# One core, a long convolution and a dilated local attention: loads as streams of their own, exchanges on two queues, another last product, another end, another order

## The chip, the core and the metric

The kernel runs on one NeuronCore of a Trainium2 chip. The metric is the device time of one execution in microseconds (us); the median of several executions counts. Five engines work side by side, each through its own list of instructions in order: PE (matrix products, with weight loads beside them), DVE and ACT (elementwise work; here above all the copies that take results out of PSUM, called evictions below), POOL (small copies, and DMAs that it issues itself), and SP, which issues nearly all DMAs. An engine that waits holds back everything behind it in its list.

## The reference, cut to what matters

```python
def reference(A_q, A_k, A_v, A_shift_k, A_ssm_k, A_ssm_D, B_x, B_wqkv, B_wo, gate_w):
    x = A_q                                         # 1 x 2048 x 640, bf16
    g = sigmoid((x * gate_w).sum(-1, keepdims=True))
    # A: four taps along the sequence, times v, then a causal convolution of length 2048 (by FFT)
    kv = shift4(A_k, A_shift_k) * A_v
    y = causal_conv(kv, A_ssm_k) + kv * A_ssm_D
    a = A_q * y
    # B: 32 heads of 20; a query sees 8 keys, 2 apart
    q, k, v = split(x @ B_wqkv)
    b = softmax_over_8(q . k * 20 ** -0.5) . v @ B_wo
    return g * a + (1 - g) * b
```

## The kernel before

Branch B: `xpose` turns eight tiles of x (PE transposes into PSUM, then copies to `xT`). `vproj` multiplies `xT` with the value weights `Wv` (L522, 170 matmuls in 34 units of five, evicted to `VW`). `qkproj` multiplies with the query and key weights `Wqk` (L569, 45 units), 128 columns at a time (`ft` = 0 to 4), evicted into two staging tiles `stg` (queries, keys). A head has 20 columns, so the rows of a head must move to other partitions: `fragger` sends them by DMA, 20 rows each, from `stg` to the tiles `qb` and `kb` (L617). These are the exchanges. Four heads make a block (t = 0 to 7, in three pairs of `qb` and `kb`, filled with mask rows by POOL copies at the start). `score_gen` multiplies a block's queries and keys (L643), ACT takes the exponential (L651, into `ETall`), `pv_gen` multiplies with `VW` (L677), DVE divides (L687, L689). `op_tr` turns the result (L853, into `oT`), `outproj` multiplies with `wo` (L869) and scales by 1 - g out of PSUM into `bl` (L874 on ACT, L876 on DVE).

Branch A: `conv` and `conv_v` do the four taps and the product with v on DVE, in steps of eight of the 64 rows that a partition holds, from row 63 down. Two parts P = 0, 1 (half the channels each) then go through a transform of 2048 = 32 x 64 points: first step `s1_unit` (L705) and second step `s2_unit` (L721, with the table `G`), once for the kernel (`h`; P = 0 into H, P = 1 into SX; input tile `h_lin`, loaded twice) and once for kv (`u`; into UC and u1). `swaps` exchanges the halves of the kernel's transform by DMA (L820), `products` multiplies on DVE (L756), `inverse1` is the first step back (L835, evicted into UC), `final` the second (L920): for each unit of `TAIL` (first tile, number of tiles) 32 small matmuls a tile into two PSUM slots, evicted into `yb`, times the gated q (L932), plus `bl` (L934), and out by DMA (L937).

PSUM has four slots of two banks; a unit of PE work takes one (some half a slot, a score group and a final unit two) and gives it back when its eviction is done.

The order is written out by hand. Each piece of the program is a generator whose `yield Req(engines, cost, deps, ...)` marks one instruction or unit; the string `ORDER` names, letter by letter, the generator that goes next, and a "-" ahead of a letter takes the second of the engines offered. Costs and due times in the requests were used to find the string; they do nothing at run time. So `ORDER` alone decides in which order each engine's list is written, and whether ACT or DVE evicts. Before, the loads after the first ones are part of `fragger` (`bulk(ft)` runs when the exchanges of `ft` have been issued); `paced` makes a load wait for a small POOL memset of its target.

SP has eight completion semaphores in turn: each of its DMAs waits until the one eight earlier has landed.

Of the kernel before, what the change touches and what calls it, by code (L numbers as in the profile page):

```python
# [10 lines left out]
BF = mybir.dt.bfloat16  # L11
# [6 lines left out]
S = 2048  # L18
# [28 lines left out]
KROWS = [(42, 64), (20, 42), (0, 20)]  # L47
TAIL = [(0, 3), (3, 3), (6, 2), (8, 3), (11, 3), (14, 2)]
LAND = dict(W0=9600.0, Wv0=5600.0, W1=23000.0, Wv1=25500.0, x=[4200.0, 7000.0, 8100.0, 10700.0, 11800.0, 12900.0, 14000.0, 15200.0], k=[20300.0])
STARTS = dict(P=5000.0, A=5000.0, D=6500.0, G=12000.0, S=18000.0)  # L50
PIPE0 = 24500.0
# [64 lines left out]
a-aa-awa-w-aw-wwww-wa-aw-wai-i-aiiai-iaa-aaai-iiffiif-iiiiifffciwicccwwfwwww-wixccccccccccccccffw-ww-wwwwccccwcccccwcccfffwwwwwwwx  # L116
ifffi-idddi-iididi-iid-idi-ididdde-iddddifffiexxfxxiffccccccccccccceffxxxxxxxxxxffeffccccccccccccccccccccccciiicdcidddx-iddfci-xd
-iidddddfffccfxedciccccdixeffdiidii-idccccccccccccccccidicccccfddxefdd-xlidexdddeffffddxxddyxeffyyccccccccccccii-iiyiddieccfddddf
-iiddfedfx-x-iiiiidddiiiiddffffffyyyyedyyxfeeexyxyccxccccyyffy-yyyifyyccccx-x-icdccccdcciddfd-iiddg-ididdde-iddidddge-iccidedcdd-i
ie-iddgdi-iiddde-iddddccccgccjejy-yyyy-yyeyyeyy-yyyy-ycyjyy-yccccccyyccclcccccjdddzdd-zdzd-zdzdj-zz-zzzjczzcz-zccddzdzz-zjzzeddddd  # L120
ezd-zz-zz-zddzdde-zeddzd-zddeddde000-0000-00p0z0z-0zz0-0000-00e0ezzz-zzzz-z010-111111-11011-0101ooo-0q111111-1r-rroorr-rr-r001ruoo
10oo-r01-111000-000001ssss1ssssss000011ssssosssosss111o1oopooo1sssu1sssss11111122oso22222222o2oo324443uu3s44s3333333334vs444444u44
444-4445-5u-u555-55u-u-uu5vv5-5555v-u-vvv-55555-vvv5-5ttstss-tsvs-vstttt-ttssststtttssststttttts-ssssstttt-tttssssttssttstsstssst
# [91 lines left out]
def kernel(  # L215
# [117 lines left out]

    def load_k(k):
# [20 lines left out]
    def load_v(c, q):  # L355
        yield from paced(f"v{q}{c}", vin[32 * q:32 * q + 32, c], raw(v2, QC * q + 80 * c, [[64 * D, 32], [D, 64], [1, 80]]), 2550.0)
# [621 lines left out]
```

## Time and profile before

| what | value |
|---|---|
| median of 3 executions | 221.87 us (221.81 to 224.73) |
| the profiled execution, whole | 222.59 us |
| its span, first to last instruction | 220.8 us |
| mean granted TensorE clock | 0.973 |
| moved by DMA | 33.40 MB, of it 19.59 MB read from HBM and 2.62 MB written |
| first exponential starts | 34.38 us |
| first output transpose (L853) starts | 151.21 us |
| first matmul of `final` (L920) starts | 196.22 us |

The last three come from the timeline. Durations of single instructions overlap a little with the next one on the same engine: two exponentials in a row take 1.86 us, one alone 0.98 us. "Busy" counts such a stretch once.

### The profile page before, as it was taken

How to read it: one execution, taken by the hardware profiler on the slowest of the kernel's cores; microseconds unless marked ns; L12 is line 12 of the kernel's file. 1: busy time of each engine (PE TensorE's matmuls, PEld its weight loads, DVE VectorE, ACT ScalarE, POOL GpSimd, SP SyncE). 2: the span in 40 equal slices, each digit the busy share in tenths (PEclk: the TensorE clock that was granted, in tenths of full speed). 3: DMA queues.
4: the chain of work that ended last, by engine and by line, in shares of the span. 5: the costliest groups of instructions: out<-in, count | busy, mean ns of one | idle time of the engine just before them, and what ended most of it. 6: DMA issues, size and time to landing. Idle time of an engine off the chain costs nothing.

```text
span 220.8 us, 8196 instructions
## 1 busy us (share of the span) xinstructions
PE 200.2 (91%) x3498; PEld 150.5 (68%) x3508; DVE 184.5 (84%) x233; ACT 174.5 (79%) x242; POOL 52.9 (24%) x130
## 2 busy tenths in 40 slices
PE   7899999999999999999967958999999999979790
PEld 3666674664656557455765747888899999968680
DVE  4556984899999999988987798997899998969782
ACT  0334448848999999989897888998799999988671
POOL 6992621470544137041600000000010000000000
PEclk9999999999999999999995599999999999999998
DMA  6999569999999999997359854026757490003545
GB/s 200 343 257 289 138 157 204 175 172 156 197 167 177 180 164 148 177 157 138 77 109 272 240 132 116 12 54 173 172 122 162 83 223 17 4 3 91 137 117 139
DMA packets 69047, 33.40 MB, mean 151 GB/s; under 512 B 51348, under 2 KB 66708, under 8 KB 69012
## 3 DMA queue, kind: packets, MB, share of 16 engines
q1 hardware_dynamic: 65684, 27.66, 60.8%
q0 software_dynamic: 2880, 4.90, 10.1%
q8 instruction: 27, 0.44, 0.9%
q10 hardware_dynamic: 448, 0.33, 0.4%
q14 instruction: 8, 0.07, 0.1%
HBM read 19.59 MB, written 2.62 MB: 101 GB/s over the span
## 4 chain that ended last, share of the span: by engine, by line
PE 61%; DVE 12%; ACT 9%; DMA 6%; issue 6%; SPq 2%; POOL 2%; ACTq 0%; DVEq 0%
PE PS L569 16%; PE PS L869 9%; PE PS L677 7%; PE PS L835 6%; PE PS L522 6%; ACT ETall L651 5%; PE PS L643 4%; DVE SX L244 4%; DVE UC L244 3%; PE PS L721 3%; PE PS L705 3%; PE PS L853 3%; DMA xn<-in_A_q_dram 2%; DMA h_lin<-in_A_ssm_k_dram 2%; PE PS L920 2%
## 5 line engine op out<-in xcount | busy, mean ns | idle before, releaser
L651 ACT ACTIVATE ETall<-PS 128x976 bf16<-128x976 f32 (+3 forms) x80 | 63.5, 859 | 6.2 <-PE PS L643 5.2
L569 PE MATMUL PS<-xT,Wqk 128*128 128x512 bf16 (+2 forms) x215 | 47.9, 356 | 1.3 <-ACT ETall L651 0.5
L569 PEld LDWEIGHTS <-Wqk 128*128 128x128 bf16 x225 | 20.8, 97 | 18.6 <-issue 0.3
L242 ACT CAST UC<-PS 128x1024 bf16<-128x1024 f32 (+2 forms) x27 | 25.6, 1013 | 1.8 <-PE PS L721 1.1
L470 DVE TENSOR_TENSOR KX<-KX 128x1280 bf16<-128x1280 bf16 x32 | 25.3, 820 | 1.6 <-DMA KX<-in_A_k_dram 1.2
L522 PE MATMUL PS<-WvT,xT 128*128 128x320 bf16 x170 | 25.8, 300 | 0.1
L869 PE MATMUL PS<-wo,oT 128*128 128x320 bf16 x160 | 24.1, 303 | 0.0
L244 DVE CAST stg<-PS 128x512 bf16<-128x512 f32 (+1 forms) x25 | 16.1, 646 | 9.1 <-PE PS L569 7.7
L617 POOL DMA_DIRECT2D qb<-stg x29 | 14.5, 503 | 35.0 <-ACT ETall L651 11.8
L617 POOL DMA_DIRECT2D kb<-stg x36 | 18.0, 508 | 19.5 <-ACT stg L242 10.1
L869 PEld LDWEIGHTS <-oT 128*128 128x128 bf16 x160 | 21.0, 145 | 1.0
L721 PEld LDWEIGHTS <-G 64*128 64x128 bf16 x512 | 18.4, 93 | 4.0 <-issue 3.2
L522 PEld LDWEIGHTS <-xT 128*128 128x128 bf16 x170 | 16.0, 98 | 7.0
L677 PEld LDWEIGHTS <-ETall 128*128 128x128 bf16 x544 | 17.5, 99 | 2.4 <-issue 0.5
L643 PE MATMUL PS<-qb,kb 31*128 31x120 bf16 (+1 forms) x544 | 16.0, 222 | 2.8 <-ACT ETall L651 1.2
L677 PE MATMUL PS<-VW,ETall 128*128 128x63 bf16 (+2 forms) x544 | 18.0, 187 | 0.6 <-ACT ETall L651 0.3
L244 DVE CAST UC<-PS 128x1024 bf16<-128x1024 f32 (+1 forms) x14 | 16.5, 1206 | 2.2 <-ACT UC L242 1.4
L643 PEld LDWEIGHTS <-kb 31*128 31x128 bf16 x544 | 9.3, 95 | 12.7 <-issue 11.3
L242 ACT CAST VW<-PS 128x320 bf16<-128x320 f32 x23 | 9.8, 432 | 9.5 <-PE PS L522 9.1
L242 ACT CAST stg<-PS 128x512 bf16<-128x512 f32 (+1 forms) x20 | 10.9, 555 | 8.0 <-PE PS L569 7.1
L244 DVE CAST SX<-PS 128x1024 bf16<-128x1024 f32 (+2 forms) x13 | 14.4, 1156 | 2.6 <-PE PS L705 2.2
L874 ACT ACTIVATE bl<-PS,omg 128x320 bf16<-128x320 f32 x31 | 15.6, 540 | 0.8 <-PE PS L869 0.3
(83 smaller groups left out, 364.4 us busy)
## 6 DMA issues: line engine op xcount, KB each, us to landing
xn<-in_A_q_dram SPq DMA_DIRECT2D x8, 320.0 KB
h_lin<-in_A_ssm_k_dram SPq DMA_DIRECT2D x16, 160.0 KB
vin<-in_A_v_dram SPq DMA_DIRECT2D x8, 320.0 KB
UC<-H SPq DMA_DIRECT2D x8, 320.0 KB
q<-in_A_q_dram SPq DMA_DIRECT2D x8, 320.0 KB
w<-SX SPq DMA_DIRECT2D x8, 320.0 KB
kb<-stg POOLq DMA_DIRECT2D x28, 85.0 KB, 5.5
out_dram<-q SPq DMA_DIRECT2D x16, 120.0 KB
```

The source lines that it names most:

```text
L242: nc.scalar.copy(dst, src)
L244: nc.vector.tensor_copy(dst, src)
L470: eng.tensor_tensor(d, kin[:, n + 3 - j:n + 3 - j + m, :], w.to_broadcast([128, m, QC]), ALU.mult)
L522: nc.tensor.matmul(ps[:, 0:320], lhsT=xT[:, dt, BQ * b:BQ * b + BK], rhs=Wv[:, dt, 320 * hp:320 * hp + 320], start=(dt == 0), stop=(dt == ...
L569: nc.tensor.matmul(ps[:, 0:n], lhsT=Wqk[:, dt, w, 128 * ft:128 * ft + 128], rhs=xT[:, dt, s0:s0 + n], start=(dt == 0), stop=(dt == NDT - 1))
L617: (nc.sync if near else nc.gpsimd).dma_start(dst[r0:r0 + rows, 0:wd], stg[fa - f0:fb - f0, 0:wd])
L643: nc.tensor.matmul(psum(g, h4 // 2)[:, h4 % 2, QB[b][0] - q0:QB[b][0] - q0 + QB[b][1]], lhsT=kb[r:r + DH + NF, BK * b:BK * b + 128], rhs=q ...
L651: nc.scalar.activation(ETall[:, e, :, 0:nq], psum(g, k)[:, :, 0:nq], ACT.Exp, scale=SCALE)
L677: nc.tensor.matmul(O[:, (b - b0) // 6, c0:c0 + 21 * nh], lhsT=ETall[:, e, hh, q0:q0 + 128], rhs=VW[:, b, 4 * t + h4:4 * t + h4 + nh, :].re ...
L721: nc.tensor.matmul(ps[:, c, 160 * jj:160 * jj + 160], lhsT=G[rows, j0 + jj, 64 - 64 * rr:192 - 64 * rr], rhs=Am[rows, rr].rearrange("p o ( ...
L869: nc.tensor.matmul(op, lhsT=oT[:, ft].rearrange("p h m a -> p a (h m)")[:, t, :], rhs=wo[:, ft, 320 * n:320 * n + 320], start=(ft == 0), s ...
L874: nc.scalar.activation(dst, op, ACT.Copy, scale=omg[:, t:t + 1])
```

## The change

Five edits and a new order.

1. The loads leave `fragger`: `bulk` is gone, and x from its third tile on, the weights, k, h, G and v are streams of their own, which `ORDER` can place. Only two tiles of x, half of `Wv` and `mm` are issued ahead of it, `mm` on SP instead of ACT. k comes in six pieces of rows instead of three. The taps' weights come in one DMA instead of four.
2. The exchanges of all but the first queries may go to POOL or SP (`Req("GS", ...)`); before, they were POOL's.
3. `final`: only the first bank of a unit (half of the 640 channels) is evicted to `yb`, by ACT, and multiplied with q afterwards. The other is multiplied with q straight out of PSUM by DVE, in place of a copy by ACT or DVE and half of the larger product.
4. `TAIL`'s last unit of two tiles becomes two units of one. Their results leave by two DMAs each, of 64 partitions, one from SP and one from ACT, in place of four.
5. `outproj` works on whole tiles: ten matmuls into one slot and one eviction of 640 columns, in place of twice five and 320.

```diff
-KROWS = [(42, 64), (20, 42), (0, 20)]
-TAIL = [(0, 3), (3, 3), (6, 2), (8, 3), (11, 3), (14, 2)]
+KROWS = [(53, 64), (45, 53), (37, 45), (29, 37), (13, 29), (0, 13)]
+FIRST = 4
+TAIL = [(0, 3), (3, 3), (6, 2), (8, 3), (11, 3), (14, 1), (15, 1)]
...
 ORDER = """
-a-aa-awa-w-aw-wwww-wa-aw-wai-i-aiiai-iaa-aaai-iiffiif-iiiiifffciwicccwwfwwww-wixccccccccccccccffw-ww-wwwwccccwcccccwcccfffwwwwwwwx
+upppqqa-aaaa-a66ap6-aapp-a6666-6i-iiiaatti-ia-aat-aiirfiiitt4ii-ii-iiit6-6fff65t6rc-cc-ccc6-6666-666ccc66666v-6f6t666-cccc6cd66idd
...
+    def load_x():
+        for a in range(2, 8):
+            yield from load(f"x{a}", xn[:, a], raw(x2, 256 * a * D, [[2 * D, 128], [D, 2], [1, D]]), 1150.0)
...
-            yield from paced(f"k{k}{q}", kin[32 * q:32 * q + 32, 3 + n0:3 + n1, :], raw(k2, n0 * D + QC * q, [[64 * D, 32], [D, n1 - n0], [1, QC]]), 62.0 * (n1 - n0))
+            yield from (paced if k >= FIRST else load)(f"k{k}{q}", kin[32 * q:32 * q + 32, 3 + n0:3 + n1, :], raw(k2, n0 * D + QC * q, [[64 * D, 32], [D, n1 - n0], [1, QC]]), 48.0 * (n1 - n0))
...
-    def bulk(ft):
...
+    def load_ks():
+        yield from load("wr", wraw.rearrange("p c j -> p (c j)"), raw(A_shift_k, 0, [[4 * QC, 4], [0, 32], [1, 4 * QC]]), 560.0)
+        for k in range(len(KROWS)):
+            yield from load_k(k)
+        yield from load_corners()
...
+    def load_h1():
+        yield from load_h(1)
...
-                    g = yield Req("G", 510.0, deps, move=28.0 * rows)
-                (nc.sync if near else nc.gpsimd).dma_start(dst[r0:r0 + rows, 0:wd], stg[fa - f0:fb - f0, 0:wd])
+                    g = yield Req("GS", dict(G=510.0, S=760.0), deps, move=28.0 * rows)
+                (nc.sync if g.eng == "S" else nc.gpsimd).dma_start(dst[r0:r0 + rows, 0:wd], stg[fa - f0:fb - f0, 0:wd])
...
-            yield from bulk(ft)
...
+            g = yield Req("P", 0.0, [ev(f"oT{ft}") for ft in range(NDT)], take=1, pe=(10, 135.0, 272.0, 133.0))
+            op = psum(g)[:, :, 0:320]
             for n in range(2):
-                g = yield Req("P", 0.0, [ev(f"oT{ft}") for ft in range(NDT)], take=1, half=1, pe=(5, 137.0, 272.0, 133.0))
-                op = psum(g)[:, 0:320]
...
-                r = yield Req("AD", dict(A=370.0, D=400.0), [g.done], give=g.banks)
-                dst = bl[:, t, 320 * n:320 * n + 320]
...
+            r = yield Req("AD", dict(A=690.0, D=790.0), [g.done], give=g.banks)
+            dst = bl[:, t].rearrange("p (n c) -> p n c", n=2)
...
-            es = []
-            for k in range(2):
-                r = yield Req("AD", n=320 * m, deps=[g.done, ybfree[n % 2]], give=[g.banks[k]])
...
-            nc.vector.tensor_tensor(reg, yb[:, 0:m, :], reg, ALU.mult)
+            a = yield Req("A", n=320 * m, deps=[g.done, ybfree[n % 2]], give=[g.banks[0]])
+            nc.scalar.copy(yb.rearrange("p t (q c) -> p q t c", q=2), pss[0][:, :, 0:160 * m].rearrange("p q (t c) -> p q t c", c=160))
...
+            hi = reg[:, :, 320:640].rearrange("p t (q c) -> p q t c", q=2)
+            nc.vector.tensor_tensor(hi, pss[1][:, :, 0:160 * m].rearrange("p q (t c) -> p q t c", c=160), hi, ALU.mult)
+            r = yield Req("D", 75.0 + 0.52 * 320 * m, [a.done])
+            nc.vector.tensor_tensor(reg[:, :, 0:320], yb, reg[:, :, 0:320], ALU.mult)
...
+            if m == 1:
+                for k, e in enumerate((nc.sync, nc.scalar)):
+                    e.dma_start(raw(outf, (32 * k + 2 * t0) * D, [[D, 2], [64 * D, 32], [1, D]]), reg[64 * k:64 * k + 64, 0])
+                continue
             for gg in range(4):
-                (nc.scalar if n == len(TAIL) - 1 and gg > 1 else nc.sync).dma_start(raw(outf, (32 * (gg // 2) + gg % 2 + 2 * t0) * D, [[64 * D, 32], [2 * D, m], [1, D]]),
+                nc.sync.dma_start(raw(outf, (32 * (gg // 2) + gg % 2 + 2 * t0) * D, [[64 * D, 32], [2 * D, m], [1, D]]),
```

What the order does is shown at three places. Names in the rows are tiles; the number behind a name tells tiles of one shape apart (stg_92 holds queries, stg_93 keys). A trailing "x4" counts rows that repeat.

ACT, up to the first exponentials (`ETall`), in the kernel before:

```order
L242 CAST stg_93<-PS 128x384 x2
L242 CAST stg_92<-PS 128x512
L242 CAST stg_93<-PS 128x512
L242 CAST VW<-PS 128x16x20 x10
L242 CAST stg_92<-PS 128x512
L651 ACTIVATE ETall<-PS 128x2x488 x2
```

The same place in the changed kernel:

```order
L244 CAST stg_93<-PS 128x384 x2
L244 CAST stg_92<-PS 128x512
L244 CAST stg_93<-PS 128x512
L244 CAST VW<-PS 128x16x20 x8
L655 ACTIVATE ETall<-PS 128x2x488 x2
L655 ACTIVATE ETall<-PS 128x2x480 x2
```

Two evictions of `VW` and one of `stg` now come after the first exponentials; on PE the first scores stand behind 80 `vproj` and 45 `qkproj` matmuls instead of 90 and 55.

SP, in the kernel before, from the last loads of v to the first swaps (`UC<-H`); `h_lin` here is the second load of the convolution's kernel, `g_nat` the way of the gate through a DMA:

```order
L326 DMA vin<-in_A_v_dram 32x64x80 x5
L326 DMA h_lin<-in_A_ssm_k_dram 32x40x64 x6
L544 DMA g_nat<-WvT 32x1x16
L326 DMA h_lin<-in_A_ssm_k_dram 32x40x64 x2
L544 DMA g_nat<-WvT 32x1x16 x3
L326 DMA SX<-cf_T 128x4x512
L820 DMA UC<-H_288 64x5x512 x2
```

The same place in the changed kernel:

```order
L622 DMA qb_81<-stg_92 8x2056
L328 DMA h_lin<-in_A_ssm_k_dram 32x40x64
L622 DMA qb_83<-stg_92 20x2056 x2
L622 DMA kb_80<-stg_93 20x2176
L622 DMA kb_82<-stg_93 20x2176 x4
L328 DMA h_lin<-in_A_ssm_k_dram 32x40x64 x7
L549 DMA g_nat<-WvT 32x1x16 x4
L824 DMA UC<-H_276 64x5x512 x2
```

The gate's DMAs now stand behind all loads of `h_lin`, and the last exchanges of the keys (`kb`) ahead of seven of the eight.

ACT at the end of the kernel before:

```order
L242 CAST yb_3512<-PS 128x2x3x160 x2
L874 ACTIVATE bl<-PS,omg 128x320 x2
L242 CAST yb_3512<-PS 128x2x3x160
L874 ACTIVATE bl<-PS,omg 128x320 x3
L242 CAST yb_3512<-PS 128x2x2x160 x2
L874 ACTIVATE bl<-PS,omg 128x320 x3
L937 DMA out_dram<-q_3296 32x2x640 x2
```

ACT at the end of the changed kernel:

```order
L930 CAST yb_3529<-PS 128x2x3x160
L930 CAST yb_3529<-PS 128x320
L878 ACTIVATE bl<-PS,omg 128x640
L942 DMA out_dram<-q_3275 2x32x640
L878 ACTIVATE bl<-PS,omg 128x640
L930 CAST yb_3529<-PS 128x320
L942 DMA out_dram<-q_3275 2x32x640
```

The store of the last unit but one now stands in ACT's list ahead of the last eviction of `bl` and the last of `yb`; the shape at the row's end, 2x32x640 in place of 32x2x640, is that of the target in HBM, outermost count first.

Elsewhere: 36 matmuls of the second transform step of u (P = 0) and their three evictions stood ahead of the first output transpose and now stand behind it; the first v load and the weights of `qkproj` stand among the first pieces of k; half of the loads of G and the constant T come later.

More of the change, by code (lines that the diff above doesn't have):

```diff
@@ L332, in paced, with load_w0, load_w1, load_wv @@
         yield from load(name, dst, src, us, [g.done])
+    def load_x():
+        for a in range(2, 8):
+            yield from load(f"x{a}", xn[:, a], raw(x2, 256 * a * D, [[2 * D, 128], [D, 2], [1, D]]), 1150.0)
+    def load_w0():
+        for w in range(2):
+            yield from load(f"W0{w}", Wqk[:, :, w, 0:128], W3[:, :, w, 0:128], 800.0)
+    def load_w1():
+        for w in range(2):
+            yield from load(f"W1{w}", Wqk[:, :, w, 128:D], W3[:, :, w, 128:D], 1900.0)
+    def load_wv():
+        yield from load("Wv1", Wv[:, :, 320:640], W3[:, :, 2, 320:640], 1400.0)
     def load_k(k):
@@ L714, in s2_unit @@
     def s2_unit(key, j0, n, Am, deps):
[L715 removed]
+        r = yield Req("P", 0.0, deps + [ev(f"G{j // 8}") for j in (j0, j0 + n - 1)], take=1, pe=(4 * n, 34.6, 70.0, 33.0))
         ps = psum(r)
```

110 lines of the change are left out of this document (43 added, 67 removed).

## The prediction

> **What bounds the kernel.** I read first the page's busy times, then the windows by stage, then the chain of waits through the middle and at the end. The line of the page gives each engine's busy time and number of instructions:
>
> ```profile
> PE 200.2 (91%) x3498; PEld 150.5 (68%) x3508; DVE 184.5 (84%) x233; ACT 174.5 (79%) x242; POOL 52.9 (24%) x130
> ```
>
> No engine is the bound everywhere, so I cut the span into stages: start, local attention, first transforms, gap, products, output with inverse, end. The columns are the stretch, its length, busy us (instructions) of PE, PEld, DVE, ACT and POOL, the granted TensorE clock, the DMA share and GB/s:
>
> ```profile
> 0.00:34.40 34.40, 31.75 (x249) 20.22 (x253) 23.77 (x36) 11.62 (x21) 20.62 (x46) 1.00 0.88 230
> 34.40:85.40 51.00, 50.13 (x737) 30.89 (x742) 45.30 (x68) 45.58 (x69) 21.40 (x53) 1.00 1.06 175
> 85.40:114.00 28.60, 27.23 (x538) 18.26 (x539) 26.70 (x35) 26.17 (x34) 9.12 (x26) 1.00 0.79 139
> 114.00:128.00 14.00, 9.98 (x212) 7.86 (x210) 10.11 (x13) 11.80 (x15) 0.38 (x2) 0.63 0.77 215
> 128.00:151.20 23.20, 20.05 (x478) 17.43 (x467) 21.10 (x23) 21.96 (x27) 0.19 (x1) 1.00 0.40 92
> 151.20:196.20 45.00, 43.60 (x711) 40.90 (x710) 40.90 (x45) 42.30 (x56) 1.23 (x3) 1.00 0.49 107
> 196.20:220.80 24.60, 17.45 (x592) 14.97 (x592) 16.64 (x17) 15.08 (x26) 0.00 (x0) 0.97 0.43 109
> ```
>
> ACT idles 22.8 us of the first 34.4, before there are scores to exponentiate. From 34.4 to 114 and from 128 to 151, DVE and ACT are busy about 90% of the time: evictions bound these. At 114 to 128 all engines have gaps and the clock is 0.63. From 151 PE leads, and the end again has gaps.
>
> **The gap: h_lin behind the gate.** The chain of waits (start, duration, what), SP's queue, and two single microseconds:
>
> ```profile
> 110.50 5.00 DMA h_lin<-in_A_ssm_k_dram
> 115.72 0.53 DVE h_lin L773
> 116.29 0.59 PE PS L705 x8
> ```
>
> ```profile
> 91.86 7.44 SPq L326 DMA_DIRECT2D h_lin<-in_A_ssm_k_dram  x6
> 108.73 0.61 SPq L544 DMA_DIRECT2D g_nat<-WvT  x1
> 109.44 2.19 SPq L326 DMA_DIRECT2D h_lin<-in_A_ssm_k_dram  x2
> 111.69 2.43 SPq L544 DMA_DIRECT2D g_nat<-WvT  x3
> ```
>
> ```profile
> 115.00:116.00 1.00, 0.00 (x0) 0.00 (x0) 0.28 (x1) 1.00 (x2) 0.00 (x0) 1.00 0.46 127
> 117.00:118.00 1.00, 0.90 (x24) 0.56 (x14) 1.00 (x1) 0.55 (x1) 0.00 (x0) 0.50 0.83 210
> 126.00:127.00 1.00, 1.00 (x29) 0.88 (x26) 0.18 (x2) 0.27 (x1) 0.00 (x0) 0.50 0.84 270
> ```
>
> Six loads are issued by 99.3, then SP waits for the gate until 108.73, so the last two loads start late, the first step waits 5 us, PE stands still around 115, and the clock is 0.50 from 117 to 127. The new order puts the gate's DMAs behind all loads: the wait goes, and with it, I take it, the low clock. What is late next is eviction. DVE and ACT have 10.11 + 11.80 = 21.9 us of work here; in the stages before and behind they are busy 95.9 of 2 x 51.8 us, 92.6% (26.70 + 26.17 + 21.10 + 21.96), so the work needs 21.9 / (2 x 0.926) = 11.8 of 14.0 us: **-2.2**. Ends: 0, if another wait takes the place; -1.9 for PE's standstill and 0.37 x 14 = 5.2 for the clock, -7.1, if PE alone were the bound.
>
> [...]
>
> **The start.** Rows: exponentials, the two PE groups put behind them, the exchange that the first scores wait for, and the exchanges by queue (count, least/median/most ns):
>
> ```profile
> 34.38 1.86 ACT L651 ACTIVATE ETall<-PS 128x976 bf16<-128x976 f32 x2
> 34.44 2.32 PE L569 MATMUL PS<-xT,Wqk 128*128 128x512 bf16 x10
> 43.95 1.52 PE L522 MATMUL PS<-WvT,xT 128*128 128x320 bf16 x10
> 29.57 4.14 DMA qb<-stg
> ```
>
> Ten matmuls of each kind fewer stand ahead of the first scores: 2.3 + 1.5 = 3.8 us of PE. The exchange takes 4.1 us to land, and SP now issues exchanges between loads, so I let the first exponential start 2.2 us earlier, at about 32.2. Ten matmuls are only moved, and DVE is full afterwards, so half passes to the end: **-1.1**. Ends: -2.2 if all passes; +4 if it goes the other way, because SP issues about ten exchanges ahead of the later pieces of k, at the 4.1 us that one takes to land, and DVE's taps stand still for that long. The taps' weights in one DMA land at most half a microsecond later, which DVE can show once: **+0.2**, ends 0 and +0.5. Six pieces of k for three are twelve more issues on SP, hidden in time in which SP only waits; without that cover each costs the 1.1 us of an issue of `h_lin` (2.19 for two).
>
> **Moved products.** Three evictions of the second step, and 36 matmuls, go from ahead of the output transposes to behind them:
>
> ```profile
> L242 ACT CAST UC<-PS 128x960 bf16<-128x960 f32 x7 | 6.6, 974 | 1.1 <-PE PS L721 1.1
> L244 DVE CAST UC<-PS 128x960 bf16<-128x960 f32 x3 | 3.4, 1155 | 0.1
> 160.18 1.51 PE PS L721 x36
> ```
>
> Ahead of it, 0.97 + 2 x 1.16 = 3.3 us of evictions are worth 3.3 / 2 / 0.92 = 1.8, with the waits about 2.1. Behind it PE is busy 43.6 of 45 and pays nearly all of the 1.51: 1.4. **-0.7**; ends -1.8 (PE's slack covers it) and +1.5 (only PE counts).
>
> **Whole-tile output projection and y times q.** Columns: engine, operation, tiles, count, busy us and mean ns, idle before:
>
> ```profile
> L874 ACT ACTIVATE bl<-PS,omg 128x320 bf16<-128x320 f32 x31 | 15.6, 540 | 0.8 <-PE PS L869 0.3
> L244 DVE CAST yb<-PS 128x960 bf16<-128x960 f32 x3 | 3.5, 1156 | 1.2 <-PE PS L920 1.2
> L689 DVE TENSOR_TENSOR VW<-PS,rd 128x960 bf16<-128x960 f32 x8 | 9.3, 1157 | 0.3
> L934 DVE TENSOR_TENSOR q<-q,bl 128x1280 bf16<-128x1280 bf16 x2 | 1.6, 824 | 0.6 <-ACT bl L874 0.6
> L756 DVE TENSOR_TENSOR H<-UC,H 128x640 bf16<-128x640 bf16 x1 | 0.5, 487 | 0.0
> ```
>
> An eviction of 976 columns takes about 0.93 (1.86 for two), so one of 640 lies between 0.54 and 0.93; at 0.7 to 0.8, sixteen for 32 save ACT 16 x (1.08 - 0.81) = 4.3 us. Nothing of it comes off: PE is the engine that is full there, with the same matmuls; but a slot is now held for ten. **0**, ends -1 and +1. The product out of PSUM is 960 columns from PSUM against SBUF, the form of the VW row: 1.157, as much as the copy (1.156) that DVE made for half of the units, and the product over the other half is about half of one of 1920 columns. DVE's work at the end stays near 16.4 against 16.64, under PE's 17.45: **0**, ends -0.6 (the idle time ahead of one `bl` product) and +0.6.
>
> **The end.** The chain, and DMA by quarter microseconds:
>
> ```profile
> 213.36 2.21 PE PS L869 x15
> 215.59 0.54 ACT bl L874
> 216.15 0.82 DVE q L934
> ```
>
> ```profile
> 217.75:218.00 0.25, 0.00 (x0) 0.00 (x0) 0.00 (x0) 0.00 (x0) 0.00 (x0) 1.00 0.62 138
> ...
> 218.75:219.00 0.25, 0.00 (x0) 0.00 (x0) 0.00 (x0) 0.00 (x0) 0.00 (x0) 1.00 0.89 308
> 219.00:219.25 0.25, 0.00 (x0) 0.00 (x0) 0.00 (x0) 0.00 (x0) 0.00 (x0) 1.00 0.07 21
> ```
>
> Before, the last sum ends at 216.97, 20.8 after this stage's start; data flow until 219.05, and the span ends 1.75 later. In the new order the last unit is one tile: its sum is 1/2 of 0.82 with the fixed part, near 0.49 (the row of 640 columns), and the matmuls of `final` come before the last of `outproj`. Laid out by these durations PE ends at 17.3 instead of 19.4. ACT then issues the store of the last unit but one, which waits for its sum at 17.45, ahead of the last `bl` (0.7 to 0.8) and `yb` (0.4); the last sum ends at 19.9. With 1.0 from issue to data (216.97 to the row of 217.75), 0.5 for 160 KB at 308 GB/s, and 1.75: 23.1 instead of 24.6, **-1.5**. Ends: -3 (without ACT's wait) and 0.
>
> **The stores.** The target of a store of one tile is written with an outermost count of 2, in place of 32. The trace has one such pattern, the gate's four DMAs (L544, outermost 2). Two quarter microseconds with nothing else in flight, and the last stores' queue (packets, MB, share of 16 engines from 216.9 to 220.8):
>
> ```profile
> 114.25:114.50 0.25, 0.14 (x10) 0.00 (x0) 0.25 (x1) 0.25 (x2) 0.00 (x0) 1.00 0.09 8
> 114.50:114.75 0.25, 0.00 (x0) 0.00 (x0) 0.25 (x1) 0.25 (x1) 0.00 (x0) 1.00 0.11 8
> q10 hardware_dynamic: 160, 0.16, 11.8%
> ```
>
> The gate's DMAs keep the share at 0.09 to 0.11, just under the 2/16 = 0.125 of two engines, and for three quarters of a microsecond. So I take two engines. Two stores of 80 KB take 0.118 x 16 x 3.9 = 7.4 us of engine time, 3.7 each. The four new stores bring 14.7; on two engines 7.4 us in a row from 18.5 (17.45 and 1.0 to data): 25.9, plus 1.75 is 27.6, against 23.1 for sixteen engines: **+4.5**. Ends: 0 (sixteen) and +6 (the last pair waits for the first to complete).
>
> [...]
>
> **Sum.** -2.2 - 1.1 + 0.2 - 0.7 + 0 + 0 - 1.5 + 4.5 = -0.8. The profiled execution took 222.59, so 221.8; it lies 0.72 above the median of 221.87, so **221.1**.
>
> **Rivals.**
>
> A, the forecast, 221.1, by itself 217.5 to 224.5: chance 0.44. The ends are those of the gap's and the stores' terms, half taken: -3.6 and +3.4.
>
> B, the stores spread over sixteen engines: 221.1 - 4.5 = 216.6. For it: a pattern of 2 x 32 rows could be split by rows, and the gate's rows are 64 bytes a piece, where an engine's share says little. Against it: 0.11 lies so close under 0.125. Chance 0.21.
>
> C, the evictions between 34 and 151 fill better, since the loads come piece by piece and exchanges have two queues. DVE and ACT idle 102.0 - 90.9 + 57.2 - 52.9 + 46.4 - 43.1 = 18.7 us there, the two added, the gap apart. With 8 of it filled, 4 us come off: 217.1 with the stores on two engines. For it: POOL issues all `kb` exchanges now,
>
> ```profile
> L617 POOL DMA_DIRECT2D kb<-stg x36: 497/498/657, 24.0 to 109.0; - x36
> ```
>
> among its copies. Against it: the queues never end last in the chain there. Chance 0.17.
>
> D, slower. SP's last key exchanges stand ahead of seven of the eight second loads of `h_lin`. If these wait for the evictions of the last `stg`, the loads start at 109 as the last two did, but seven at 1.1 us each. The first step then waits 3 us more than before, PE stands still for more than the 1.9 us of now, and the clock is 0.50 for at least 10 us again. Then the -2.2 is not had and 3 us come on top: 221.1 + 2.2 + 3 = 226.3. It decides from the point where the last `h_lin` lands over 3 us later than the products of v are through; under that it is A. For it: the exchange row, which runs until 109.0. Against it: exchanges of the block before are free earlier, and POOL shared the work. Chance 0.18.
>
> [...]
>
> **Chances.** A measurement of this kernel tells about 2% from no change, so from 217.4 to 226.3 is "the same". Faster: B and C where they come in whole, 0.20 + 0.14, 0.34. Slower: D's upper half and the bounds of A, 0.17. The same: 0.49. The range takes in B and C below (216.6 less 1 for the bounds of the start) and D's middle above: 215.5 to 226.0.
>
> **What would show it.** A clock of 1.00 at 105 to 127 and no `h_lin` DMA in the chain: the first term. A first exponential at 32 to 33: the start. The final stage from its first L920 to the end near 27.6, with a DMA share near 0.125 for 7 us: the stores; a share near 0.9 for half a microsecond: B. ACT's store ahead of its last `bl`, with idle time: the end's -1.5. A stretch at 0.50 behind an `h_lin` DMA: D. The forecast is wrong if the share at the end is high, or if idle time of DVE and ACT between 34 and 151 halves.

## The result and the profile after

The changed kernel takes 233.14 us in the median (233.12 to 237.03), beside 222.37 us for the kernel before on the same chip (221.81 to 224.73): 1.046 times as long, with an interval of 1.037 to 1.056. The ratios here and below leave out executions over 1.5% longer than the fastest of the same kernel. The forecast was 221.1 and no measurable change. The profiled execution of the changed kernel has a span of 231.4 us, 10.6 more than before.

The page's line of busy times shows that the work itself did not grow:

```profile
PE 204.5 (88%) x3508; PEld 150.9 (65%) x3508; DVE 181.1 (78%) x235; ACT 169.9 (73%) x228; POOL 36.7 (16%) x97
```

DVE and ACT are 8.0 us less busy together, and yet the span is longer, so it is waiting that came in. (PE's 4.3 us more come with ten matmuls whose records the trace of the kernel before lacks, and with 17.1 us at half clock before its last matmul in place of 10.2.) The windows of the changed kernel by stage say where (stretch, length, busy us of PE, PEld, DVE, ACT and POOL, clock, DMA share, GB/s):

```profile
0.00:32.05 32.05, 29.41 (x233) 18.68 (x234) 15.10 (x23) 11.12 (x19) 18.52 (x32) 1.00 0.89 221
32.05:47.40 15.35, 15.17 (x187) 8.92 (x187) 13.61 (x19) 13.45 (x22) 5.03 (x16) 1.00 0.93 189
47.40:57.00 9.60, 6.30 (x62) 2.96 (x63) 4.00 (x8) 3.69 (x4) 0.15 (x2) 0.64 1.04 158
57.00:111.00 54.00, 53.53 (x838) 31.65 (x839) 49.12 (x72) 48.89 (x73) 10.16 (x34) 1.00 0.72 139
111.00:131.00 20.00, 15.53 (x419) 12.04 (x416) 17.46 (x20) 19.19 (x26) 1.41 (x8) 1.00 0.52 93
131.00:144.80 13.80, 12.36 (x250) 10.95 (x250) 10.41 (x12) 11.71 (x15) 0.38 (x2) 0.63 0.92 218
144.80:156.00 11.20, 10.02 (x192) 8.71 (x191) 11.20 (x11) 11.16 (x13) 0.19 (x1) 1.00 0.74 160
156.00:202.50 46.50, 44.97 (x756) 42.33 (x755) 43.20 (x53) 38.64 (x44) 0.87 (x3) 1.00 0.47 108
202.50:219.93 17.43, 17.19 (x592) 14.69 (x592) 15.39 (x21) 10.97 (x14) 0.00 (x0) 1.00 0.42 107
219.93:231.40 11.47, 0.00 (x1) 0.00 (x0) 1.64 (x4) 1.11 (x2) 0.00 (x0) 0.66 0.25 71
```

The ends of the stretches are milestones that both kernels have. Beside each other:

| stretch | before | after | difference |
|---|---|---|---|
| start to the first exponential | 34.4 | 32.05 | -2.35 |
| to the first output transpose (151.2; 156.0) | 116.8 | 123.95 | +7.15 |
| to the first matmul of `final` (196.2; 202.5) | 45.0 | 46.5 | +1.5 |
| to PE's end (215.6; 219.93) | 19.4 | 17.43 | -2.0 |
| to the end of the span | 5.2 | 11.47 | +6.3 |

Two places carry it: the 9.6 us from 47.4 to 57, and the end behind PE.

**47.4 to 57.** The same window of the kernel before:

```profile
47.40:57.00 9.60, 9.37 (x106) 5.18 (x106) 9.07 (x15) 7.90 (x13) 2.11 (x12) 1.00 1.01 178
```

DVE and ACT did 17.0 us of work there before and 7.7 after; until 47.4 the two kernels had done nearly as much (54.5 and 53.3, by the same counts). Shared between the two engines, the 9.3 us that are missing make 4.7, an estimate of what this window costs, against the net 4.8 us (-2.35 + 7.15) by which the output transposes come later. PE's timeline of the changed kernel shows the wait (start, duration, line, shape, count, idle before it and what ended that):

```profile
44.50 2.20 PE L527 MATMUL PS<-WvT,xT 128*128 128x320 bf16 x15 [0.17 <-ACT ETall L655]
46.53 0.70 PE L681 MATMUL PS<-VW,ETall 128*128 128x63 bf16 x20
47.16 0.23 PE L647 MATMUL PS<-qb,kb 31*128 31x128 bf16 x2
50.63 0.59 PE L647 MATMUL PS<-qb,kb 31*128 31x128 bf16 x14 [3.24 <-DMA kb<-stg]
```

L647 are the scores of the second block. Two of their sixteen matmuls run, then PE waits 3.24 us for an exchange of keys. Its clock is 0.50 from 49.5 to 56.3, 6.8 us. The same place on PE before:

```profile
46.38 0.70 PE L677 MATMUL PS<-VW,ETall 128*128 128x63 bf16 x20
46.93 3.56 PE L522 MATMUL PS<-WvT,xT 128*128 128x320 bf16 x25
50.33 1.24 PE L569 MATMUL PS<-xT,Wqk 128*128 128x512 bf16 x4
51.50 0.39 PE L643 MATMUL PS<-qb,kb 31*128 31x128 bf16 x16
```

There, 25 `vproj` and some `qkproj` matmuls stood between, and the scores began at 51.5 without a wait. Between 36 and 56 us an exchange of keys landed 2.4 to 5.8 us after its issue before, and 5.5 to 6.3 after: somewhat slower, but above all it was covered before.

**The end.** The chain of waits of the changed kernel behind the last matmul, and half microseconds of its DMA share (last but one number; GB/s last):

```profile
219.86 0.49 DVE q L939
220.35 0.41 DVE q L934
220.77 0.76 ACTq L942
...
221.70 0.57 issue
222.27 0.43 ACT yb L930
...
223.07 0.49 DVE q L939
```

```profile
224.50:225.00 0.50, 0.00 (x0) 0.00 (x0) 0.00 (x0) 0.00 (x0) 0.00 (x0) 0.50 0.13 49
...
229.00:229.50 0.50, 0.00 (x0) 0.00 (x0) 0.00 (x0) 0.00 (x0) 0.00 (x0) 0.50 0.14 51
229.50:230.00 0.50, 0.00 (x0) 0.00 (x0) 0.00 (x0) 0.00 (x0) 0.00 (x0) 0.50 0.08 31
```

The sum of the last unit but one (the first row) ends at 220.35. ACT issues the store of that sum (until 221.53) ahead of its last two evictions, and the last sum ends at 223.56. Data then flow for six microseconds at a share of 0.13, as much as two engines of sixteen (0.125).

**The middle.** No `h_lin` DMA is in the chain any more, but a clock of 0.50 is there again, from 131.4 to 141.6, as long (10.2 us) as in the kernel before (116.9 to 127.1):

```profile
131.00:131.50 0.50, 0.09 (x3) 0.09 (x4) 0.50 (x1) 0.50 (x2) 0.00 (x0) 0.89 0.94 209
131.50:132.00 0.50, 0.50 (x12) 0.45 (x13) 0.32 (x1) 0.50 (x1) 0.00 (x0) 0.50 0.94 186
```

### The profile page after: what moved, and what is told of

The parts are those of the page before. It is cut to its first block, busy times and chain, and to the rows that moved or that the text cites. A ratio compares the mean times of both kernels' runs of the same rounds, so it can differ in the third digit from the quotient of the medians.

```text
span 231.4 us, 8236 instructions
## 1 busy us (share of the span) xinstructions
PE 204.5 (88%) x3508; PEld 150.9 (65%) x3508; DVE 181.1 (78%) x235; ACT 169.9 (73%) x228; POOL 36.7 (16%) x97
## 4 chain that ended last, share of the span: by engine, by line
PE 62%; DVE 10%; DMA 8%; issue 6%; ACT 5%; SPq 3%; POOL 1%; ACTq 0%; DVEq 0%; POOLq 0%
PE PS L574 16%; PE PS L873 9%; PE PS L839 8%; PE PS L527 6%; PE PS L725 5%; PE PS L681 5%; DMA kb<-stg 4%; PE PS L647 4%; PE PS L709 3%; PE PS L857 2%; ACT ETall L655 2%; DMA xn<-in_A_q_dram 2%; PE PS L924 2%; DMA qb<-stg 2%; DVE u L246 2%
## 5 line engine op out<-in xcount | busy, mean ns | idle before, releaser
L655 ACT ACTIVATE ETall<-PS 128x976 bf16<-128x976 f32 (+3 forms) x80 | 64.4, 865 | 12.6 <-PE PS L647 12.3
L574 PEld LDWEIGHTS <-Wqk 128*128 128x128 bf16 x225 | 20.8, 98 | 19.2 <-issue 1.6
L527 PE MATMUL PS<-WvT,xT 128*128 128x320 bf16 x170 | 27.0, 308 | 0.2 <-ACT ETall L655 0.2
L244 ACT CAST stg<-PS 128x512 bf16<-128x512 f32 (+1 forms) x30 | 15.8, 553 | 9.6 <-PE PS L574 9.3
L647 PE MATMUL PS<-qb,kb 31*128 31x120 bf16 (+1 forms) x544 | 17.0, 222 | 5.5 <-DMA kb<-stg 3.8
L873 PEld LDWEIGHTS <-oT 128*128 128x128 bf16 x160 | 21.1, 145 | 1.0
L647 PEld LDWEIGHTS <-kb 31*128 31x128 bf16 x544 | 9.2, 95 | 16.7 <-issue 11.1
L622 POOL DMA_DIRECT2D qb<-stg x18 | 9.0, 504 | 58.9 <-ACT stg L244 26.2
L244 ACT CAST u<-PS 128x960 bf16<-128x960 f32 (+2 forms) x17 | 15.6, 990 | 1.9 <-PE PS L725 1.9
L246 DVE CAST UC<-PS 128x1024 bf16<-128x1024 f32 (+1 forms) x13 | 15.2, 1204 | 2.1 <-PE PS L839 1.1
L878 ACT ACTIVATE bl<-PS,omg 128x640 bf16<-128x640 f32 x14 | 11.2, 820 | 5.8 <-PE PS L873 3.5
L246 DVE CAST VW<-PS 128x320 bf16<-128x320 f32 x12 | 5.8, 490 | 12.3 <-PE PS L527 12.3
L693 DVE TENSOR_TENSOR VW<-PS,rd 128x960 bf16<-128x960 f32 (+1 forms) x16 | 13.9, 866 | 0.6
```

Source lines behind the costliest of these rows:

```text
L244: nc.scalar.copy(dst, src)
L246: nc.vector.tensor_copy(dst, src)
L527: nc.tensor.matmul(ps[:, 0:320], lhsT=xT[:, dt, BQ * b:BQ * b + BK], rhs=Wv[:, dt, 320 * hp:320 * hp + 320], start=(dt == 0), stop=(dt == ...
L574: nc.tensor.matmul(ps[:, 0:n], lhsT=Wqk[:, dt, w, 128 * ft:128 * ft + 128], rhs=xT[:, dt, s0:s0 + n], start=(dt == 0), stop=(dt == NDT - 1))
L647: nc.tensor.matmul(psum(g, h4 // 2)[:, h4 % 2, QB[b][0] - q0:QB[b][0] - q0 + QB[b][1]], lhsT=kb[r:r + DH + NF, BK * b:BK * b + 128], rhs=q ...
L655: nc.scalar.activation(ETall[:, e, :, 0:nq], psum(g, k)[:, :, 0:nq], ACT.Exp, scale=SCALE)
```

## The experiments

Each kernel was timed beside the kernel before on the same chip; the ratio is to that. The middle of one and the same order scatters: the first matmul of `final` started at 201.1 to 204.3 in the profiled executions of e1, e2, e3, e7 and the changed kernel, which differ little ahead of it. In the kernel before, b1 and e13, whose order is the same up to the last stage, the first exponential started at 34.4 to 36.6 and the first output transpose at 151.2 to 153.3. So differences of 1 us between two experiments are not read, and single stretches are read from a profile where the mechanism is seen in it.

### The stores

**b1_count2**, the kernel before with the new pattern alone:

```diff
+            if n == len(TAIL) - 1:
+                for k, e in enumerate((nc.sync, nc.scalar)):
+                    for tt in range(m):
+                        e.dma_start(raw(outf, (32 * k + 2 * (t0 + tt)) * D, [[D, 2], [64 * D, 32], [1, D]]), reg[64 * k:64 * k + 64, tt])
+                continue
```

> The kernel before, with only the last unit's four stores written with an outermost count of 2 in the target, the same four DMAs of 80 KB on the same queues. Theory: 14.7 us of engine time on two engines is 7.4 us of data in place of 1.1, so +6.2: about 228.3, share 0.13 at the end. Rival (the pattern does not matter): 222.

Measured: ratio 1.034 (1.022 to 1.046), +7.5 us of 223.15. One of the microseconds in which nothing but these stores runs:

```profile
222.00:223.00 1.00, 0.00 (x0) 0.00 (x0) 0.00 (x0) 0.00 (x0) 0.00 (x0) 0.50 0.13 47
```

The last sum ends at 218.5 and the span at 229.9, 11.4 us later; before it was 3.8. Same bytes, same number of DMAs, same queues: the pattern costs it. These 7.6 us are 1.4 more than the working gave; what the rest is was not looked into.

**e1_rows32**, the reverse:

```diff
-            if m == 1:
-                for k, e in enumerate((nc.sync, nc.scalar)):
-                    e.dma_start(raw(outf, (32 * k + 2 * t0) * D, [[D, 2], [64 * D, 32], [1, D]]), reg[64 * k:64 * k + 64, 0])
-                continue
             for gg in range(4):
-                nc.sync.dma_start(
+                (nc.scalar if m == 1 and gg > 1 else nc.sync).dma_start(
```

> The changed kernel, but the stores of the two one-tile units leave by four DMAs of 32 rows each (outermost count 32), two from SP and two from ACT, as the last unit's did before. Theory (two engines carry the new stores; data flowed at a DMA share of 0.13 from 224.0 to 229.5): the tail after the last sum falls from 7.8 us to about 3.5, total 233.1 - 4.3 = about 228.8, share near 0.9 for half a microsecond at the end. Rival (the end is long because of ACT's wait and the completion, not because of the pattern): 232 to 234, and no change in the DMA share.

Measured: 1.035 (1.024 to 1.045), 230.15 us; 3 us less than the changed kernel, between theory and rival. In the profile the last sum ends at 225.15 and the span at 228.6, so 3.45 us in place of 7.84, and the last data flow at

```profile
226.00:226.50 0.50, 0.00 (x0) 0.00 (x0) 0.00 (x0) 0.00 (x0) 0.00 (x0) 0.50 0.63 167
```

The 4.4 us of the end are there. In this profile `final` began 1.8 us later than in the changed kernel (204.3 beside 202.5), within the scatter of the middle, which hides the rest.

**e3_both** has no store in ACT's list ahead of its last evictions (and the edit of e2; the lines are shown against e1):

```diff
-                (nc.scalar if m == 1 and gg > 1 else nc.sync).dma_start(
+                (nc.scalar if t0 == 15 and gg > 1 else nc.sync).dma_start(
```

> Both edits at once, and the store of the last unit but one is issued by SP alone, so that ACT's last two evictions wait for no store. Theory: 233.1 - 4.3 (stores) - 4 to 6 (exchange) - 2 (ACT's wait ahead of its last bl) = 221 to 223, about the kernel before. Rival (the rest of the new order is slower by itself, DVE's taps end at 110 instead of 92): the sum of the first two and no more than that, 225 or above.

Measured: 1.019 (1.008 to 1.029), 227.23 us. The rival's value. The last sum now ends 1.6 us behind PE instead of 3.4 in e1, but the span ends 5.0 behind that sum, since SP issues until 223.06:

```profile
215.67 7.39 SPq L941 DMA_DIRECT2D out_dram<-q  x11
```

**e7_tail3** gives two of these stores to POOL (`nc.gpsimd if t0 == 14 and gg > 1`).

> As e3_both, but two of the four stores of the last unit but one are issued by POOL, which has nothing else to do there. Theory (in e3_both SP issues stores until 223.1, 2.7 us after the last sum, and so sets the end): 1.0 to 1.5 us come off, tail from the last sum 3.5 to 4. Rival (POOL's DMAs land later than SP's): no change or 1 us more.

Measured: 1.015 (1.008 to 1.022), 226.86 us; from the last sum to the end 4.1 us in place of 5.0. As expected in the profile, not to be told apart in the time.

### The exchange that PE waits for

**e2_kb_on_sp**: one "-" in the order, which takes SP for one exchange:

```diff
-...fcfccc4-cc-cddc-ce7...
+...fcfcc-c4-cc-cddc-ce7...
```

> The changed kernel, but one exchange of keys (12 rows to the second pair, the one PE waits for at 50.6) is issued by SP instead of POOL; nothing else. Theory (it was held in POOL's queue behind an exchange of queries that waits for the first scores to end at 44.6): PE's idle time at 47.4 to 50.6 and the clock of 0.50 until 56.3 both vanish, and 4 to 6 us come off: 227 to 229. Rival 1 (evictions bound the stretch behind it, so the time is lost again further on): PE's gap goes, the total stays at 232 to 233. Rival 2 (the exchange is late for another reason, its data or its landing): gap and total stay.

Measured: 1.045 (1.035 to 1.055), 232.13 us: as slow as the changed kernel, so rival 2. PE's gap is still there:

```profile
47.40 0.23 PE L647 MATMUL PS<-qb,kb 31*128 31x128 bf16 x2
50.00 0.87 PE L647 MATMUL PS<-qb,kb 31*128 31x128 bf16 x14 [2.37 <-issue]
```

In the changed kernel POOL issued this exchange at 45.13, and it landed 5.46 us later. Here SP starts its five at 43.37, 1.8 us earlier, and the scores go on 0.6 us earlier. The theory of POOL's queue falls: an exchange of keys took 5.5 to 6.8 us to land at this place, whichever queue issued it, while k and v were loaded with a DMA share of 0.5 to 1.4. What is left is that the scores stand too close behind it in PE's list; e8 tests that.

**e5_cover** puts two `vproj` and two `qkproj` units between:

```diff
-...cc-cddc-ce7-7ddifd7dff-7-cdfdd-iiiiffdtd...
+...cc-c7-7i-i7-7iiddc-ceddfddff-cdfddiffdtd...
```

> The third kernel (stores of 32 rows, no store ahead of ACT's last evictions, the one exchange of keys on SP), and in the order of PE two vproj and two qkproj units put ahead of the second block's first scores. Theory (the exchange lands 5.5 to 6.5 us after its issue on either queue, as in the kernel before, and what was lost is the PE work that stood in front of the scores there: 25 vproj and 10 qkproj matmuls before, 15 vproj now): the gap of 2.4 to 3.2 us at 47 to 50.6 and the clock of 0.50 behind it both go, 3 to 5 us come off: 222 to 224. Rival (evictions bound, lost again further on): the gap goes, the total stays at 226 to 228.

Measured: 1.032 (1.024 to 1.039), 230.01 us: not faster than e3, by the medians slower. The long gap and the low clock at 47 to 57 are gone, but the time is not had. The chain of waits there:

```profile
44.33 5.43 DMA qb<-stg
49.94 0.70 DVE stg L246
50.69 0.85 PE PS L527 x5
52.11 1.25 PE PS L574 x5
```

A `qkproj` unit is evicted into a staging tile that exchanges of the same round are still reading (the chain names one of queries), so these units wait for what they were to cover, and everything behind them on DVE and PE as well. The scores began at 53.3.

**e8_vproj** puts five `vproj` units there, which need no staging tile, as the kernel before had them (and the division of the first block ahead of their evictions). Some of them are taken from further on in the order, which the shortened lines do not show:

```diff
-...cc-cddc-ce7-7ddifd7dff-7-cdfdd-iiii...
+...cc-ce7-77-7777777ddc-cddifddff-cdfdd-iiii...
```

> As e3_both, with five vproj units (25 matmuls, none of which needs the exchanges or their staging tiles) put ahead of the second block's first scores in the order, as they stood in the kernel before. e5_cover put qkproj units there, and they waited for the staging tile until the same exchange had landed. Theory (what was lost at 47 to 57 is independent work as a cover for the exchange): no gap, no half clock, the second transform stages start 2 to 4 us earlier, 223 to 225. Rival (the middle of the new order is bound by something further on; starts of the last stage lay at 201.1 to 204.3 in all kernels so far, with the gap or without): 226 to 228.

Measured: 1.019 (1.011 to 1.026), 226.13 us, beside 227.23 for e3. The window of this kernel:

```profile
47.40:57.00 9.60, 8.14 (x103) 4.46 (x101) 6.96 (x11) 7.01 (x11) 0.00 (x0) 1.00 1.00 155
```

DVE and ACT do 14.0 us of work there (8.3 in e3, 7.7 in the changed kernel), the clock stays at 1.00, and the output transposes begin at 152.7 (154.6 in e3, 156.0 in the changed kernel). The time is the rival's value. The ratio equals that of e3 (1.0187 and 1.0186), and the medians differ by 1.1 us, which is not read here. The stretch is mended; that it shortens the kernel is not shown.

**e9_vproj_taps** adds six of DVE's tap instructions (`f`) there.

```diff
-...cc-ce7-77-7777777ddc-cddifddff-cdfdd-iiii...
+...cc-c7e-7f7-7f77f77f77ffddc-cddidd-cddd-iiii...
```

> As e8_vproj, and six of DVE's tap instructions, 4.9 us, moved ahead into the time in which DVE waits there (it stood still from 48.3 to 52.7). Theory (DVE and ACT had done 10.5 us less by 57 than in the kernel before, and the stretches after 111 are bound by their evictions): another 1 to 2 us below e8_vproj. Rival: the same as e8_vproj.

Measured: 1.022 (1.015 to 1.029), 227.03 us. The rival's value: no gain.

**e10_before_bare** does the reverse on the kernel before: its five `vproj` units (`x`) behind the second block's first scores.

```diff
-...ceffxxxxxxxxxxffeffccccccccccccccccccccccciiicdcidddx...
+...ceffffeffccccccccccccccccccccccciiicdciddxxxxxxxxxxdx...
```

> The kernel before, with its five vproj units at 47 to 50.5 put behind the second block's first scores, so that these stand uncovered as in the changed kernel; nothing else. Theory (cover): PE idles 2.5 to 3.5 us at 47 to 51, the clock falls to 0.50 for 6 to 7 us, and 3 to 6 us are added: 225 to 228. Rival (evictions bound, the vproj units are made up for later): the gap appears, the total stays at 222 to 223.

Measured: 1.020 (1.013 to 1.027), 226.92 us: 4.4 us more by the ratio, within what the theory gave. But the mechanism of the theory is not to be seen. PE in the only trace, that of the longest execution (231.8 us):

```profile
49.39 0.38 PE L643 MATMUL PS<-qb,kb 31*128 31x128 bf16 x13 [0.44 <-DMA kb<-stg]
49.70 1.25 PE L569 MATMUL PS<-xT,Wqk 128*128 128x512 bf16 x5
52.39 0.84 PE L522 MATMUL PS<-WvT,xT 128*128 128x320 bf16 x5 [1.43 <-DVE VW L689]
53.75 1.26 PE L522 MATMUL PS<-WvT,xT 128*128 128x320 bf16 x5 [0.52 <-ACT VW L242]
55.53 1.49 PE L522 MATMUL PS<-WvT,xT 128*128 128x320 bf16 x5 [0.52 <-ACT VW L242]
```

PE waits 0.44 us for the exchange of keys, not 2.5 to 3.5. Its longer waits stand ahead of the moved units, which now come in a row: each but the first waits for the eviction of the one before, and the clock is 0.50 from 54.0 to 60.9 (0.84 over 47.4 to 57, 0.93 over 57 to 85). The mean clock of the other four executions (0.966 to 0.982) is no lower than in the kernel before on that chip (0.965 to 0.980), so a further 6.8 us at half clock is not seen in them. So the place of these 25 matmuls is worth 2.0% to the kernel before; that it is worth it as a cover for the exchange is not shown.

### The start, the gate and the new end by themselves

**e6_taps**: the last quarters of k's second piece ahead of the first exchanges, six tap instructions earlier.

```diff
-...rc-cc-ccc6-6666-666ccc66666v-6f6t666-cccc6cd66idd -6dddiiiiiittidt...
+...rttc-cc-ccc6-6666-666ccc66666v-6ffff6666-cccc6cd6 6iddfff-6dddiiiiiitidt...
```

> As e5_cover, and the last two quarters of k's second piece are loaded ahead of the first exchanges on SP, with six of DVE's tap instructions moved ahead of evictions for which DVE waits before 33 us. Theory (DVE did 8.7 us less in the start than before, and evictions bound what follows): some 4 us of DVE's work move into its idle time, worth about 2 us, less up to 1 us by which the first exchanges start later: 1 us below e5_cover. Rival (the two loads delay the first scores by as much as is gained): the same as e5_cover, first exponential 1 us later.

Measured: 1.029 (1.019 to 1.040), 229.84 us, as e5. The first exponential starts at 31.8 as in e5, so the loads do not delay it, and the taps bring nothing that can be measured.

**e11_gate_behind**: one letter (`j`) of the order of the kernel before is moved.

```diff
-...yyyy-ycyjyy-yccccccyy...
+...yyyy-ycyyy-yccccjccyy...
```

> The kernel before, with the gate's first DMA put behind the last two loads of h_lin in SP's list, as the changed kernel has it; nothing else. Theory of the prediction's first term: the last two loads start about 9 us earlier, the 5.0 us wait for h_lin, PE's standstill at 114.4 to 116.3 and the clock of 0.50 until 127 all go, 2.2 us come off: 219.7 beside 221.9. Rival (the gate itself is then late and its product, or the evictions, take the gap's place; in the changed kernel the clock fell at 131 without any h_lin wait): 221 to 223, and a stretch at 0.50 stays.

Measured: 0.998 (0.993 to 1.002), 223.04 us: between 1.5 us less and 0.5 us more than before. SP's list shows that the edit does what it should, eight loads in a row and the gate behind:

```profile
92.16 11.45 SPq L326 DMA_DIRECT2D h_lin<-in_A_ssm_k_dram  x8
108.33 2.64 SPq L544 DMA_DIRECT2D g_nat<-WvT  x4
```

No `h_lin` DMA is in the chain. Yet PE is no fuller, and the clock falls again, here from 117.6 to 124.4. (The mean clock of this execution is 0.979, that of the profiled one of e14, with the same order up to there, 0.959, so the shorter stretch is not a gain to count on.)

```profile
114.00:116.00 2.00, 0.96 (x26) 0.70 (x28) 1.32 (x3) 1.91 (x4) 0.00 (x0) 1.00 0.07 17
116.00:118.00 2.00, 0.87 (x28) 0.71 (x29) 1.96 (x2) 2.00 (x3) 0.00 (x0) 0.89 0.95 215
118.00:120.00 2.00, 1.74 (x32) 1.51 (x30) 1.42 (x2) 2.00 (x3) 0.19 (x1) 0.50 0.78 206
```

DVE and ACT are busy from 116 on and PE waits for them. The chain now runs through DVE's evictions of H, until 114.4, and the first step begins at 114.99 in place of 116.29: 1.3 us earlier, though the wait for `h_lin` had 5.0 in the chain. The wait that was named there was one of several that ended close together.

**e13_new_end**: the kernel before with edits 3 and 4 alone; its stores as in e7, outproj in halves, the last 14 letters rewritten for two units of one tile.

> The kernel before, with edits 3 and 4 alone: half of y times q out of PSUM, the last unit in two of one tile, their stores in four DMAs of 32 rows (two of the first by POOL); outproj stays in halves and the order ahead of the last unit is untouched. Theory (the last stage of the changed kernel, from its first matmul to PE's end, took 17.4 us in place of 19.4, and its end was spoilt by the stores): 1 to 2.5 us come off, 219.5 to 221. Rival (the 2.0 us came from the new order and from whole-tile evictions, not from these edits): 221.5 to 223.

Measured: 1.004 (0.999 to 1.009), 224.8 us. The rival. From the first matmul of `final` to PE's end the profile has 18.3 us (198.3 to 216.7) instead of 19.4, and to the last sum 19.4 instead of 20.8. Nothing of it arrives: the stores' data end by 219.8, but the span at 223.7. Between the two the trace has a single DMA packet, at 221.6, of a queue of instructions:

```profile
q14 instruction: 1, 0.01, 0.2%
```

Whether the end waits for that packet is not shown; if it does, the 1.4 us up to the last sum are hidden by it in this execution.

**e14_gate_psum**: e11 and edit 3, with the last unit as before.

> The kernel before with two parts of the change: the gate's first DMA behind the last loads of h_lin, and half of y times q out of PSUM in all units; the last unit of two tiles and its stores as before. Theory (the profile of e11_gate_behind reached the output transposes 1.9 us earlier, the last stage gains up to 1 us by the product out of PSUM): 1 to 2.5 us come off, ratio 0.99 to 0.995. Rival (the low clock only moves, and the end is bound by PE and the stores): 0.998 to 1.003.

Measured: 0.999 (0.995 to 1.003), 222.54 us. The rival: no version here is measurably faster than the kernel before.

**e15_repaired**: the changed kernel with all repairs, e7's stores and e8's order.

> The changed kernel with the three repairs together: stores of 32 rows, the last unit but one issued by SP and POOL, the exchange of keys on SP and five vproj units ahead of the second block's first scores. Theory (repairs add up: e8_vproj less 0.9 us of SP's stores at the end): 225 to 225.5, ratio 1.008 to 1.015, still slower than the kernel before because DVE's taps and the stretches with a clock of 0.50 are as in the changed kernel. Rival (with the repairs the new order is as fast): 222 to 223.5.

Measured: 1.011 (1.006 to 1.017), 225.44 us. As the theory had it: the repairs bring back 7.7 of the 10.8 us by the medians, and 1.1% stay. Most of this comes from the stores and ACT's wait: e7, with the same stores and without the five units, is at 1.015, and the intervals of the two overlap.

## Why the prediction was wrong, step by step

Of the sum, by the profiled executions, what lies behind the output transposes came within 1.4 us (forecast +1.4 - 2.1 + 5.1, measured +1.5 - 2.0 + 6.3), and what lies ahead of them was wrong by 10 us (forecast -5.2, from -2.2, -1.1, +0.2 and the -2.1 of the moved evictions; measured -2.35 + 7.15 = +4.8).

- **The step that failed: the -5.2 ahead of the transposes.** It has two parts. The prediction put PE's wait for the later exchanges at nothing, without a reason, and it passed on gains at places where other work was as late (the next three points).
- **The exchanges, put at nothing.** The first exponential came at 32.05 (forecast 32.2). But the prediction counted the exchanges only up to the first scores. It did not ask what stands between an exchange and the scores of the next block in the new order, though its own row gave 4.1 us from issue to landing. There the cover fell from 25 `vproj` matmuls to 15, PE waited 3.24 us and ran at half clock for 6.8. The wait stands in the profiles of the changed kernel (3.24 us) and e2 (2.37), and the low clock in those of the changed kernel and e3 (0.64 over 47.4 to 57) and of e2 (0.50 from 50 to 51). In e8 no exchange is in the list of PE's waits from 44 to 58, and the clock is 1.00 over 47.4 to 57 in e8 and e9 and over the first 57 us in e15, so the missing cover is shown as their cause. With it back, the output transposes began at 152.7 to 154.9, without it at 154.6 to 157.8, in the mean 2.3 us later. What of this reaches the end is not shown: e8 takes as long as e3, and e15 is 0.4% under e7, within the intervals.
- **The start: half passes to the end, -1.1.** "Ten matmuls are only moved" was taken for half a gain. The early start had to be paid: DVE had done 15.1 us of work by the first exponential instead of 23.77. By 47.4 most of it was made up (DVE 4.2 us behind, ACT 3.0 ahead), and taps moved forward brought nothing (e6, e9). For the +0.2 of the taps' weights no row was given; DVE's first copy of them began at 18.12 in place of 18.80 and waited for no DMA.
- **The gap, -2.2.** The wait for `h_lin` went as forecast and the clock's stretch did not; it lies at 131.4 to 141.6. By itself the edit is worth between 1.5 us gained and 0.5 lost (e11), so the term was too large: PE, DVE and ACT wait for one another there, and a wait that ends together with others is worth little. "What is late next is eviction" was right. The 92.6% taken from the neighbouring stages was not reached: DVE and ACT are busy 91.6% of 111 to 131, and 80% of 131 to 144.8, where the clock is low.
- **Moved products.** The price behind the first transpose was 1.4 in the forecast and 1.5 in the stage. The gain ahead of it cannot be seen among the rest.
- **Whole-tile output projection and y times q.** The product out of PSUM brought no gain in time by itself (e14) or with the units of one tile (e13), as forecast. The whole-tile projection was not run by itself; its eviction of 640 columns took 0.82 us (forecast 0.7 to 0.8). The last stage to PE's end took 17.43 (forecast 17.3).
- **The end, -1.5.** ACT's wait was seen and sized too small. From the sum that the store reads to ACT's next eviction the forecast's durations leave about 0.4 us; it was 1.2 (220.35 to 221.57), since the issue alone took until 221.53, and the eviction that feeds the last product came after that. The last sum ended 3.6 us behind PE (forecast 2.6; 1.6 in e3, without the store there) and 21.1 us after the stage's start instead of 19.9.
- **The stores, +4.5.** Right in place and size: 4.4 in e1's profile (2.6 by the ratios, with the scatter of the middle in it). The gate's rows, with a share of 0.09 to 0.11, were enough to see it. That two engines carry such a store is an estimate from this share (2/16 = 0.125). The measured shares agree: the last stores ran at a share of 0.13 to 0.14 in the changed kernel and of 0.12 to 0.14 in b1, and with 32 rows at 0.55 to 0.63 in e1. By what rule a store is spread over engines is not shown.
- **Rival D** had the right kind of place, a wait of PE behind late exchanges with the clock behind it, and put it at the second loads of `h_lin`. There the last exchanges of keys did land late (issued at 111.4, used at 116), but PE had other work, and waited 0.5 us. Seven loads of `h_lin` were issued behind them, from 115.1 to 122.35, later than D had them, and nothing in the chain waited for them: DVE first used `h_lin` at 129.07, straight behind other work. So D's delay came about and its wait did not.

Not settled: the 1.1% that e15 keeps. In its profile the output transposes begin 2.7 us later than before (153.9 beside 151.2, or beside the 151.2 to 153.3 of the three profiles of that order), the stage up to `final` is 1.4 longer, the last stage to PE's end 1.4 shorter, and the end 0.5 longer. By 57 its DVE and ACT have done 68.5 us, against 71.4 before and 61.0 in the changed kernel. Which part of the order ahead of the transposes holds the rest was not tried.

## What to carry to other kernels

When an order is rewritten, list for each transfer what independent work stands between its issue and its first reader, before and after, and set that against the landing times of the old trace; cover that reads or fills the same staging tile is none (in e5 PE still waited 1.0 us for that tile's eviction). Read the outermost count of every DMA pattern, above all of the last stores, where nothing hides them (2 in place of 32 made the kernel before 7.5 us slower in b1). And a wait that ends a chain is worth its length only if the engines beside it were not about to wait as well (in e11, a wait of 5.0 us left the chain and the next step began 1.3 us earlier): ask what each of them would have done in that time.

## What the runs showed of the hardware

The clock fell at 131.4 without any long gap. PE was busy 11.4 of the 15 us ahead of it, by the window:

```profile
116.00:131.00 15.00, 11.36 (x306) 8.58 (x307) 12.79 (x16) 14.20 (x19) 0.00 (x0) 1.00 0.55 89
```

The longest of its waits there, by the list of waits (total, times, longest):

```profile
PE PS L709 <- DVE rd L691: 0.6, 1, 0.6
```

The low clock then held for 10.2 us. At 47.4, in one gap of 3.2 us, the clock fell 2.1 us after the gap began and came back 5.7 us after it had ended. In e5 the longest of PE's waits from 40 to 62 was 1.2 us, and the clock was 1.00 over the first 111 us. What makes the clock fall or come back is not shown by these.

With an outermost count of 2 the last stores of the changed kernel moved 49 to 51 GB/s in rows of 1280 bytes, with stores of SP's and of ACT's queue in flight. The last stores of the kernel before, with a count of 32, moved 138 and 308 GB/s in two quarter microseconds that the prediction shows.
